# Fewer up products in the last three blocks: 20 matrix products for four column blocks, chained in PSUM banks

## The chip, the cores and the metric

The kernel runs on one core of one Trainium2 chip. The metric is the device time of one execution in microseconds (us). TensorE (PE) multiplies matrices into PSUM, VectorE (DVE) and ScalarE (ACT) read PSUM and work in SBUF, GpSimd (POOL) helps, and SyncE (SP) issues the DMA transfers. PSUM has eight banks of 512 fp32 values per partition.

## The reference

A gated linear attention with a state per head, and behind it a multiplicative feed-forward network on its result:

```
q, k, v, f_logit: (4, 8, 768, 48) float32
f = sigmoid(f_logit)
state = f[t] * state + k[t] (outer) v[t]        # 48 x 48 per head
y[t]  = q[t] @ state
x = y laid out as 3072 tokens x 384
a = x @ w1;  b = x @ w2                         # 384 -> 1024, w1 and w2 float64 in memory
h = (a * b) @ w3                                # 1024 -> 1024
out = h @ w_out                                 # 1024 -> 384
```

The kernel multiplies `w3 @ w_out` once into `wc` (1024 x 384), so that the network is an **up product** of x with w1 and w2, an elementwise product of the two results, and a **down product** with `wc`. All matmuls are fp32.

## The kernel before

The 3072 tokens are six blocks (`NB`, index `n`) of 512 tokens (`TB`). The attention runs in 24 chunks of 128 tokens and delivers each block's x as `xt`: three slices of 128 of the 384 input features (`KM`), by 512 tokens. The up product of a block fills `ab` (the product a * b): eight column blocks of 128 (`KF`) of the 1024 outputs. The down product of a block is two calls of `down(i)`, of 28 matmuls each, in seven runs of four.

**The order of all work is made by a planner.** `Plan.add` takes an engine, a cost, what is waited for and a priority; `Plan.order` goes through the tasks as a list scheduler and puts out one instruction stream per engine. Tasks can take a place from a pool: `f` is a pool of PSUM banks (`NF` = 4), given back when the tasks that end its use are done. The attention holds the other four banks, as two tiles of two banks each, `pa` and `py`. Each engine executes its stream in order.

**How an up product is done.** Block 0 is multiplied plainly (`part`). Blocks 1 to 5 use `seven(jc)`, called four times per block for the column blocks `jc` and `jc + 4`: the tokens are two halves of 256 (`TH`), and a scheme of the Strassen kind takes 11 products of 128x128 by 128x256 in place of 12, in seven groups `m1` to `m7`. Each product is done for w1 and w2 (`both_`, line 901), which land side by side in the two halves of one bank. So a seven has 22 matmuls. `sums` makes four sums of parts of x (VectorE, line 875), and `w12t` holds sums of weights. The results are joined like this (X, Y, Z are banks):

```
m1 -> X;  k1: a = X (ScalarE copy, line 914)
m6 -> Y;  u2 = Y + a (VectorE, line 935);  m2 added to X
k11: ScalarE copies half of X (line 938), e11: VectorE multiplies it by the other half (line 941)
m7 added to Y;  u3 = Y + a (line 935)
m5 -> Z;  c22: u3 += Z (line 953);  e22 (line 956)
m4 added to Y;  c21: a += Y;  e21.   m3 added to Z;  c12: u2 += Z;  e12
```

The `e` steps multiply the w1 half by the w2 half and write `ab`. The down products are lines 805 (matmuls), 1032 (four sums `S0` to `S3`), 1039 to 1083 (copies and adds) and a store of two tiles (line 1088).

**Work that fills ScalarE late.** `ranges` (lines 1309 to 1343) looks at all weights once more after the attention has ended: 34 loads of 512 KB, each followed by two ScalarE passes with a sum (lines 1325 and 1329), at the lowest priority. The verdict on them is awaited by the very last group of matmuls (`m3` of the last `down`).

Of the kernel before, what the change touches and what calls it, by code (L numbers as in the profile page):

```python
# [84 lines left out]
AHEAD = 22.0  # L85
HEAVY = 3
WITH_POOL = 0.6
QLATE = 0.1
FLOOR = 2.0**-60
RANGE = 2.0**-40  # L90

# [139 lines left out]
def ranged(ctx, tc, q, k, f_logit, v, w1, w2, w3, w_out, out, ident, w12, wc, left):  # L231
# [13 lines left out]
    ps = ctx.enter_context(tc.tile_pool(name="ps", bufs=1, space=PSUM))  # L245
    ps_f = ctx.enter_context(tc.tile_pool(name="ps_f", bufs=1, space=PSUM))

    floor = keep.tile([R, NQ], F32, name="floor")
    spare = keep.tile([P, NQ], F32, name="back")
    back = spare[0:R]  # L250
    gate = [keep.tile([R, NQ + 1], F32, name=f"gate{i}") for i in range(2)]
    qs, ks, fs = ([keep.tile([R, NQ], F32, name=f"{nm}{i}") for i in range(n)] for nm, n in (("q", 3), ("k", 2), ("f", 2)))
    both = keep.tile([P, 2 * WIDE], F32, name="A")
    flat = [both[:, i * WIDE : i * WIDE + WIDE] for i in range(2)]
    masked = [t.rearrange("p (r h c) -> p r h c", r=2, h=HP) for t in flat]
# [32 lines left out]
    qs.append(at(12288, NQ)[0:R])  # L288
    dns = {nm: at(12288 + DH * i, DH) for i, nm in enumerate(("m1", "u2", "u3"))}

    plan = Plan()
    plan.pool("f", NF)
    plan.slot("a", 2)
    plan.slot("lane", 8)
    plan.slot("heavy", HEAVY)
    plan.slot("ab", 4)
# [2 lines left out]

    def bank():  # L300

        return ps_f.tile([P, TB], F32, name=f"f{plan.got}")

    def idle(n):

# [80 lines left out]
    def front(u):  # L386

        s, t = st[u], tk[u]
        n0 = need(u)
        ask = n0 - 30 if u in (0, 1) or u > 3 else turn_of(str(u))  # L390
        ask = [ask, ask + 0.5, ask + 1.0, n0 - (28.2, 28.2, 28.2, 28.2, 12)[min(u, 4)] if u in (0, 1) or u > 3 else ask + 1.2]

        def load(dst, src):
            def emit():
                if dst is fs[0] and u == 0:

                    nc.sync.dma_start(dst[0:64], src[u].rearrange("two d n -> (two d) n")[0:64])
                    nc.sync.dma_start(dst[rows(1)], src[u, 1])
                    return
                for par in range(2):  # L400
                    nc.sync.dma_start(dst[rows(par)], src[u, par])  # L401
            return emit

        fu, qu, ku = (x[u if u < 4 else u % n] for x, n in ((fs, 2), (qs, 3), (ks, 2)))

        def free(n, *names):

            if u < 4:
                return []
            return asked[8:9] + [tk[u - n if u - n >= 4 else u % n][nm] for nm in names]  # L410

        since = n0 - AHEAD if 4 < u < 8 else 0.0
        t["lf"] = moves(2, 197, 300, load(fu, f_logit), free(2, "g"), ask[0], since=since)
        t["lk"] = moves(2, 197, 300, load(ku, k), free(2, "k"), ask[1], since=since)
        t["lq"] = moves(2, 197, 300, load(qu, q), free(3, "q"), ask[2], since=since)

        def load_v():
            s["v"] = at(12288 + NQ, DM) if u == 3 else loads.tile([P, DM], F32, name="vt")
            loaded(s["v"], u)

        t["lv"] = moves(
            1, 197, 320, load_v, [] if u == 3 else past(u, 4 if u in (4, 5, 6) else 3, "v", "s"),
            ask[3],
        )

        def gates():
            nc.scalar.activation(gate[u % 2][:, 0:NQ], fu, AF.Sigmoid)  # L427

        t["g"] = plan.add("ACT", 0.65, gates, [t["lf"]] + past(u, 2, "r") + past(u, 3, "G"), n0)
        if u % NCH and "G" in tk[u - 1]:  # L430
            tk[u - 1]["G"]["deps"].append(t["g"])

        def forward():
            s["P"] = one.tile([R, NQ], F32, name="fwd")
            nc.vector.tensor_tensor_scan(s["P"], gate[u % 2][:, 0:NQ], floor, 0.0, ALU.mult, ALU.max)  # L435

        t["p"] = plan.add("DVE", 1.25, forward, [t["g"]] + past(u, 1, "q", "i", "l"), n0)

        def last():
            nc.scalar.copy(lasts[:, u], heads(s["P"])[:, :, C - 1])  # L440

        t["l"] = plan.add("ACT", 0.2, last, [t["p"]], n0)

        def ends():
            nc.vector.reciprocal(heads(back)[:, :, C - 1], heads(s["P"])[:, :, C - 1])

        t["i"] = plan.add("DVE", 0.18, ends, [t["p"]] + past(u, 1, "r"), n0)

        def scale_q():
            s["Q"] = work3.tile([R, NQ], F32, name="Q")  # L450
            nc.vector.tensor_tensor(s["Q"], qu, s["P"], ALU.mult)

        t["q"] = plan.add("DVE", 0.72, scale_q, [t["p"], t["lq"]] + past(u, 3, "v", "a"), n0 + QLATE, shared=True)

        def backward():
            s["R"] = one.tile([R, NQ], F32, name="bwd")
            nc.vector.tensor_tensor_scan(  # L457
                s["R"][:, ::-1], gate[u % 2][:, NQ:0:-1], back[:, ::-1], 0.0, ALU.mult, ALU.max
            )

        t["r"] = plan.add("DVE", 1.25, backward, [t["i"]] + past(u, 1, "k"), n0)

        def scale_k():
            s["K"] = work.tile([R, NQ], F32, name="K")
            nc.vector.tensor_tensor(s["K"], ku, s["R"], ALU.mult)  # L465

        t["k"] = plan.add("DVE", 0.72, scale_k, [t["r"], t["lk"]] + past(u, 2, "a", "t"), n0, shared=True)
        if u in (2, 3):
            t["k"]["frees"].append(coming)
# [207 lines left out]
    def rest(u):  # L677
# [68 lines left out]
                t["b"] = plan.add("ACT", 0.75, blocks, [t["d"]] + past(u, 1, "v"), n0)  # L746

        def outcome():
            s["ys"] = work3.tile([R, HP, C], F32, name="ys")
            py = s["yb"] if u < NPE else s["py"][0:R, :, 0 : 2 * C]  # L750
            ys = s["ys"]
            if u >= NPE:
# [44 lines left out]


    blk = [{} for _ in range(NB)]
    stores, upq, downq = [], [], []  # L800

    def three(out_, lhs, rhs, start=True):

# [6 lines left out]
    def ffn(n):  # L810
# [69 lines left out]
        def seven(jc):  # L880
# [26 lines left out]
                return a_b(jc + half * KH)[:, tok * TH : tok * TH + TH]  # L907

            def m1():
                both_("X", [wt(0, 0)], [quarter(0, 0)], True)  # L910

            def k1():
                q["a"] = firsts[q["no"] % 2]
                nc.scalar.copy(q["a"], q["X"])

            def m6():
                both_("Y", [tw(1)], [xs()[:, 1]], True)

            def m5():
                both_("Z", [tw(0)], [xs()[:, 0]], True)  # L920

            def m2():
                both_("X", [wt(1, 0), wt(2, 0)], [quarter(1, 0), quarter(2, 0)])

            def m7():
                both_("Y", [tw(2), wt(2, 1)], [xs()[:, 2], quarter(2, 1)])
# [4 lines left out]
            def m3():  # L931
                both_("Z", [wt(1, 1), wt(2, 1)], [xs()[:, 3], quarter(2, 0)])

            def u(nm):
                return lambda: nc.vector.tensor_tensor(ups[nm], q["Y"], q["a"], ALU.add)  # L935

            def k11():
                nc.scalar.copy(to(0, 0), q["X"][:, 0:TH])  # L938

            def e11():  # L940
                nc.vector.tensor_tensor(to(0, 0), q["X"][:, TH:TB], to(0, 0), ALU.mult)

            def first():
                return q["a"]

            def second():
                return ups["u2"]

            def third():
                return ups["u3"]  # L950

            def ended(bank_, more):
                return lambda: nc.vector.tensor_tensor(more(), q[bank_], more(), ALU.add)  # L953
# [15 lines left out]

            ready = [tk[n * UB + c]["x"] for c in range(UB)]  # L970
            begin = takes_ab(jc, plan.add("PE", 0.0, lambda: None, ready + [s["S", 3]] + old(1, "m7"), n0))
            pe("m1", one_, m1, [begin], 0, takes=["f"])
            q["k1"] = plan.add("ACT", 0.57, k1, [q["m1"]], -200, takes=["a"])
            pe("m6", one_, m6, [q["m1"]], -1, takes=["f"])
            pe("m5", one_, m5, [q["m6"]], -1, takes=["f"])
            dve("u2", 0.69, u("u2"), [q["k1"], q["m6"]] + old(1, "e12"))
            pe("m2", two_, m2, [q["k1"], q["m6"]], -5)
            q["k11"] = plan.add("ACT", 0.38, k11, [q["m2"]], -200)
            dve("e11", 0.43, e11, [q["m2"], q["k11"]], frees=[q["m1"]])
            pe("m7", two_, m7, [q["u2"], q["m2"]], -5)  # L980
            dve("u3", 0.69, u("u3"), [q["m7"]] + old(1, "e22"))
            dve("c22", 0.69, ended("Z", third), [q["u3"], q["m5"]])
            dve("e22", 0.43, times(1, 1, third), [q["c22"]])
            pe("m4", two_, m4, [q["u3"]], -6)
            dve("c21", 0.69, ended("Y", first), [q["m4"]], frees=[q["m6"]])
            dve("e21", 0.43, times(1, 0, first), [q["c21"]], frees=[q["k1"]])
            pe("m3", two_, m3, [q["c22"], q["m4"]], -6)
            dve("c12", 0.69, ended("Z", second), [q["m3"]], frees=[q["m5"]])
            dve("e12", 0.43, times(0, 1, second), [q["c12"]])
            s["done"][place_of(jc) // KH].extend([q["e11"], q["e22"], q["e21"], q["e12"]])  # L990
            s["up"] += [q[nm] for nm in ("m1", "m2", "m7", "m4", "m3")]

        if n == 0:
            part(0, 2, range(KH))
            part(2, 4, range(KH))
            part(0, 2, range(KH, KF))
# [312 lines left out]
    def ranges():  # L1309
# [19 lines left out]
            return lambda: nc.scalar.activation(a, a, AF.Sign, bias=small, accum_out=counts[:, i : i + 1])  # L1329

        for i in range(n):
            ld = moves(1, LOOK, 400, load(i), last[:1] if i < 2 else last[i - 1 : i], 500 + i, SURE_W)
            a = plan.add("ACT", 0.92, total(i), [ld], 500 + i)
            last.append(plan.add("ACT", 0.95, count(i), [a], 500 + i))

# [40 lines left out]
    for u in range(NU):  # L1376
# [11 lines left out]
        if u == 3:  # L1388
            folding()
        if u == NU - 1:  # L1390
            weighed = [ranges()] if wide else []
            looked = plan.add("DVE", 1.0, judge, [tk[i]["y"] for i in range(NU)] + weighed, -20)
            sent = moves(1, 0.4, 250, told, [looked], 0, 20.0)
# [400 lines left out]
```

## Time and profile before

| what | value |
|---|---|
| median of 3 runs | 474.16 us (473.37 to 476.61) |
| the profiled execution, own time | 473.17 us |
| its span, first to last instruction | 471.4 us |
| mean granted TensorE clock | 0.999 of full |
| TensorE busy | 463.6 us, 98% |
| VectorE busy | 347.0 us, 74% |
| ScalarE busy | 170.2 us, 36% |
| GpSimd busy | 65.5 us, 14% |
| rows of line 901 (sevens' matmuls) | 400 + 240 + 160 + 80 = 880 |
| start of the first look, end of the last (lines 1325, 1329) | about 268 us, 401.6 us |

How to read it: a span is the time from the first to the last instruction. A row of a group names a line of the kernel, the engine, the operation, the output tile and the input tiles, the shapes, how many there were, their busy time and the mean of one in nanoseconds, and then how long the engine had been idle before them and for whom. One fp32 matmul of the program is two MATMUL rows in the trace, and rows of successive matmuls overlap, so that a busy time or a mean is not the rate; the chain of work that ended last gives the rate, as time per row of a stretch without a gap.

The order of the stages by the chain: the attention's start with block 0's up product until 67 us, the fold of w3 and w_out between attention steps until 117 us, the attention with down and up products of blocks 0 and 1 until 264 us, and then only up and down products, block by block.

### The profile page before, as it was taken

What the parts mean: (1) busy time and instruction counts of PE and PEld (TensorE: products, weight loads), DVE (VectorE), ACT (ScalarE), POOL (GpSimd) and SP (SyncE); (2) the same over time, 40 slices, a digit from 0 to 9 for tenths busy, and PEclk for the clock granted to TensorE, in tenths of its full rate; (3) what the DMA queues carried; (4) which work ended last, traced back from release to release, by engine and by line L of the source; (5) the groups of instructions that cost most, each with busy time, mean ns of one, the idle gap of its engine ahead of it and who ended that gap; (6) DMA issues with size and microseconds to landing.
All of it is one profiled execution on the core that took longest, in us unless ns stands there. A gap on an engine that the chain in (4) does not pass through costs nothing.

```text
span 471.4 us, 11711 instructions
## 1 busy us (share of the span) xinstructions
PE 463.6 (98%) x4848; PEld 405.3 (86%) x4848; DVE 347.0 (74%) x615; ACT 170.2 (36%) x398; POOL 65.5 (14%) x90
## 2 busy tenths in 40 slices
PE   8999999999999999999999999999999999999996
PEld 6778885666999888889998889988899888989995
DVE  8998999999898999999986556436672457555541
ACT  4555433432234433233333335454444464200000
POOL 9330000222132332033231000000000000000000
PEclk9999999999999999999999999999999999999999
DMA  6998897643356654164441445554454542000011
GB/s 181 287 293 296 289 346 271 199 117 88 84 150 170 207 140 128 55 186 121 123 116 26 117 137 198 167 171 145 128 194 153 182 136 89 1 0 1 35 66 40
DMA packets 43164, 68.74 MB, mean 146 GB/s; under 512 B 5201, under 2 KB 28242, under 8 KB 42082
## 3 DMA queue, kind: packets, MB, share of 16 engines
q1 hardware_dynamic: 43106, 67.95, 46.3%
q8 instruction: 39, 0.64, 0.6%
q14 instruction: 19, 0.16, 0.1%
HBM read 58.88 MB, written 9.04 MB: 144 GB/s over the span
## 4 chain that ended last, share of the span: by engine, by line
PE 95%; DVE 1%; SPq 1%; DMA 1%; issue 0%; POOL 0%; POOLq 0%; DVEq 0%
PE f L901 41%; PE f L805 32%; PE f L1254 9%; PE py L562 3%; PE pa L488 2%; PE pa L595 2%; PE py L581 2%; PE f L502 2%; PE f L308 1%; SPq L401 1%; DMA ab<-in_k_dram 1%; DVE K L465 0%; PE f L783 0%; DVE bwd L457 0%; DVE fwd L435 0%
## 5 line engine op out<-in xcount | busy, mean ns | idle before, releaser
L901 PE MATMUL f<-xt,w 128*128 128x256 f32 x400 | 103.3, 380 | 0.0
L901 PEld LDWEIGHTS f<-xt,w 128*128 128x128 f32 x400 | 75.4, 190 | 10.0
L901 PE MATMUL f<-place 128*128 128x256 f32 x240 | 63.4, 380 | 0.0
L618 POOL TENSOR_SCALAR_AFFINE_SELECT A<-A 64x512 f32<-64x512 f32 (+1 forms) x46 | 42.5, 924 | 109.2 <-ACT A L612 107.1
L805 PE MATMUL f<-place 128*128 128x192 f32 x288 | 51.2, 328 | 0.0
L901 PEld LDWEIGHTS f<-place 128*128 128x128 f32 x240 | 45.0, 190 | 6.0 <-ACT kt L636 0.2
L805 PEld LDWEIGHTS f<-place 128*128 128x128 f32 x288 | 47.1, 190 | 0.5 <-issue 0.2
L935 DVE TENSOR_TENSOR place<-f,a 128x512 f32<-128x512 f32 x40 | 27.6, 690 | 22.6 <-PE f L901 20.7
L1254 PE MATMUL f<-place 128*128 128x384 f32 x128 | 42.7, 488 | 0.0
L805 PE MATMUL f<-xt,w 128*128 128x256 f32 x192 | 42.1, 380 | 0.0
L805 PEld LDWEIGHTS f<-xt,w 128*128 128x128 f32 x192 | 36.3, 190 | 5.0
L901 PE MATMUL f<-xt,place 128*128 128x256 f32 x160 | 38.1, 381 | 0.0
L1254 PEld LDWEIGHTS f<-place 128*128 128x128 f32 x128 | 23.8, 190 | 15.3
L805 PE MATMUL f<-wc,ab 128*128 128x192 f32 x192 | 35.4, 327 | 0.0
L953 DVE TENSOR_TENSOR place<-f,place 128x512 f32<-128x512 f32 x40 | 27.6, 689 | 9.1 <-PE f L901 8.5
L901 PEld LDWEIGHTS f<-xt,place 128*128 128x128 f32 x160 | 30.0, 190 | 3.9
L805 PEld LDWEIGHTS f<-wc,ab 128*128 128x128 f32 x192 | 31.9, 190 | 0.5
L435 DVE TENSOR_TENSOR_SCAN fwd<-gate,floor 112x512 f32<-112x512 f32 x24 | 31.4, 1307 | 1.3 <-ACT gate L427 0.2
L457 DVE TENSOR_TENSOR_SCAN bwd<-gate,back 112x512 f32<-112x512 f32 x24 | 29.7, 1237 | 0.7
L953 DVE TENSOR_TENSOR a<-f,a 128x512 f32<-128x512 f32 x20 | 13.8, 689 | 21.0 <-PE f L901 21.0
L938 ACT COPY ab<-f 128x256 f32<-128x256 f32 x20 | 7.4, 372 | 58.8 <-PE f L901 58.8
L1329 ACT ACTIVATE A<-A,back 128x512 f32<-128x512 f32 x34 | 26.3, 772 | 1.0
(134 smaller groups left out, 705.8 us busy)
## 6 DMA issues: line engine op xcount, KB each, us to landing
A<-in_w_dram SPq DMA_DIRECT2D x28, 512.0 KB, 4.3
place<-in_w_dram SPq DMA_DIRECT2D x8, 1024.0 KB, 6.4
place<-in_w_dram SPq DMA_DIRECT2D x12, 512.0 KB, 6.7
out_dram<-o SPq DMA_DIRECT2D x24, 192.0 KB, 2.1
q<-in_q_dram SPq DMA_DIRECT2D x46, 96.0 KB, 3.1
vt<-in_v_dram SPq DMA_DIRECT2D x23, 192.0 KB, 3.0
k<-in_k_dram SPq DMA_DIRECT2D x44, 96.0 KB, 2.7
yt<-ys SPq DMA_DIRECT2D x44, 96.0 KB, 2.8
```

Of the source, the lines that this page charges most:

```text
L435: nc.vector.tensor_tensor_scan(s["P"], gate[u % 2][:, 0:NQ], floor, 0.0, ALU.mult, ALU.max)
L457: nc.vector.tensor_tensor_scan(s["R"][:, ::-1], gate[u % 2][:, NQ:0:-1], back[:, ::-1], 0.0, ALU.mult, ALU.max)
L488: nc.tensor.matmul(s["pa"][half * W : half * W + W, par, hp * W : hp * W + W], lhsT=s["K"][rows(par), cols], rhs=s["Q"][rows(par), cols], ...
L502: nc.tensor.transpose(out=s["pk"][:, hp // 2, hp % 2 * R : hp % 2 * R + R], in_=s["K"][:, hp * C : hp * C + C], identity=ident[0:R, 0:R],)
L562: done = nc.tensor.matmul(y_block(u, hp, par, half)[p0 : p0 + w], lhsT=s["v"][half * W : half * W + W, h * D : h * D + w], rhs=s["A"][half ...
L618: nc.gpsimd.affine_select(out=a, in_=a, pattern=pattern, compare_op=ALU.is_ge, fill=0.0, base=0, channel_multiplier=-1,)
L805: nc.tensor.matmul(out_, lhsT=lhs[i], rhs=rhs[i], start=start and i == 0, stop=i == len(lhs) - 1, skip_group_check=True,)
L901: nc.tensor.matmul(q[nm][:, which * TH : which * TH + TH], lhsT=lhs[i](which), rhs=rhs[i], start=start and which == 0 and i == 0, stop=i = ...
L935: return lambda: nc.vector.tensor_tensor(ups[nm], q["Y"], q["a"], ALU.add)
L953: return lambda: nc.vector.tensor_tensor(more(), q[bank_], more(), ALU.add)
L1254: nc.tensor.matmul(w3s["p", jc], lhsT=w3s[jc][:, kc * P : kc * P + P], rhs=wos[:, kc], start=(kc == 0), stop=(kc == KF - 1),)
L1329: return lambda: nc.scalar.activation(a, a, AF.Sign, bias=small, accum_out=counts[:, i : i + 1])
```

## The change

Three things change.

1. **Blocks 3, 4 and 5** (`n >= MANY`, `MANY` = 3) use a new `many(g)` in place of `seven`, called for two groups `g` of four column blocks each. It is a scheme of 20 products for (2 token halves) x (3 feature slices) x (4 column blocks), where a plain product has 24. Each is again done for w1 and w2, so a group has 40 matmuls and a block 80, where four sevens have 88. It needs 12 sums of parts of x per block (`X_SUMS`, VectorE, 128x256), 22 sums of weights once (`W_SUMS`, VectorE, 128x512), 12 sums of products per group (`Y_SUMS`, VectorE, 128x512) and 8 ends per group (`Y_ENDS`). The 20 products stand in six **chains** (`CHAINS`): the products of a chain are added one on the other in one bank, and where a partial sum is needed by itself, ScalarE copies the bank (`keep_`) before the next product of the chain is added; 12 copies per group. One end per group is read from the bank: a half copy by ScalarE and a multiplication by VectorE.
2. **The sevens** of blocks 1 and 2 are chained likewise: `m1` starts bank Y, ScalarE copies it (`k1`), `m6` is added and copied (`u2`), `m7` is added and copied (`u3`), `m4` is added. `m2` starts bank X and `c11` adds the kept m1. So the two additions `u2` and `u3` by VectorE become copies by ScalarE, `m6` waits for `k1`, and the slot `a` has one place.
3. **Space.** The weight sums and kept products live in tiles that the attention has left (`homes`: floor, gates, q, k, f, and the working tiles), which get 128 partitions for it. A task `over` gathers the ends of the attention: the weight sums wait for it. After the attention the banks of `pa` and `py` join the pool `f` (`plan.pools["f"] += [late] * 4`), each bank being a half of one of the two tiles.

`LOOKS`, `W_SINCE` and `W_STEP` are 0 and change nothing by themselves; the planner's costs on TensorE are as before (0.86 for two matmuls). The core of the diff:

```diff
+MANY = 3
+CHAINS = [
+    [(3, 0), (4, 4), (4, 23)],
+    [(0, 13), (1, 6), (1, 26)],
+    [(5, 8), (9, 25), (6, 17), (10, 31)],
+    [(8, 28)],
+    [(11, 14), (12, 22), (3, 19)],
+    [(7, 10), (16, 21), (14, 12), (15, 32), (17, 30), (0, 33)],
+]
...
     def bank():
+        if plan.got >= NF:
+            nm = ("pa", "py")[(plan.got - NF) // 2]
+            if nm not in found:
+                found[nm] = ps.tile([P, 2, NQ], F32, name=nm)
+            return found[nm][:, plan.got % 2]
         return ps_f.tile([P, TB], F32, name=f"f{plan.got}")
...
             def m1():
-                both_("X", [wt(0, 0)], [quarter(0, 0)], True)
-            def k1():
-                q["a"] = firsts[q["no"] % 2]
-                nc.scalar.copy(q["a"], q["X"])
+                both_("Y", [wt(0, 0)], [quarter(0, 0)], True)
+            def m2():
+                both_("X", [wt(1, 0), wt(2, 0)], [quarter(1, 0), quarter(2, 0)], True)
             def m6():
-                both_("Y", [tw(1)], [xs()[:, 1]], True)
+                both_("Y", [tw(1)], [xs()[:, 1]])
-            def u(nm):
-                return lambda: nc.vector.tensor_tensor(ups[nm], q["Y"], q["a"], ALU.add)
+            def kept(to_):
+                return lambda: nc.scalar.copy(to_(), q["Y"])
...
+        def many_sums():
+            for k, (i, o, j, h) in enumerate(W_SUMS if not w_nodes else []):
...
+                w_nodes.append(plan.add("DVE", 0.69, emit, [over] + w_nodes[-1:], 100 * MANY + W_LATE + k, since=W_SINCE + W_STEP * k))
+            for k, (i, o, j, h) in enumerate(X_SUMS):
...
+                s["X", k] = plan.add("DVE", 0.43, emit, before + x_task(i) + x_task(j), 100 * n + 30 + k)
...
+        def many(g):
...
+            def product(t, c, first, a, b):
+                def emit():
+                    if first:
+                        banks[g, c] = bank()
+                    for which in range(2):
+                        lhs = up_weights(w12, which, b // 4, column(b % 4, g)) if b < 4 * KM else w_view(b)[:, which, g]
+                        nc.tensor.matmul(
+                            banks[g, c][:, which * TH : which * TH + TH], lhsT=lhs, rhs=x_node(a),
+                            start=first and which == 0, stop=True, skip_group_check=True,
+                        )
+                return emit
...
+            for c, chain in enumerate(CHAINS):
+                last = None
+                for m, (a, b) in enumerate(chain):
+                    deps = [begin] + x_task(a) + ([w_nodes[b - 4 * KM]] if b >= 4 * KM else []) + ([last] if m else opened[-1:])
+                    task[t] = last = plan.add("PE", 0.86, product(t, c, m == 0, a, b), deps, n0 + 0.1 * c - 0.01 * m, takes=["f"] if m == 0 else [])
...
+                    if t in kept:
+                        def keep_(t=t, c=c):
+                            where_[t] = temporary(plan.got)
+                            nc.scalar.copy(where_[t], banks[g, c])
+                        last = plan.add("ACT", 0.57, keep_, [last], n0 - 200, takes=["t"], frees=[opener] if t in ends_of else [])
...
-        if n == 0:
+        if n >= MANY:
+            for g in range(2):
+                many(g)
+        elif n == 0:
...
         if u == NU - 1:
+            late = plan.add("none", 0.0, lambda: None)
+            plan.pools["f"] += [late] * 4
+            for nm in ("y", "mid", "m", "v"):
+                tk[u][nm]["frees"].append(late)
+            over["deps"] += [tk[u][nm] for nm in ("z", "v", "mid", "k", "q", "y")] + [tk[u - 1]["z"]]
```

## The prediction

> **What bounds the kernel now.** I read the page's busy shares first, then the chain that ended last, then busy time by 12 us stretches, and only then single rows. The page:
>
> ```profile
> PE 463.6 (98%) x4848; PEld 405.3 (86%) x4848; DVE 347.0 (74%) x615; ACT 170.2 (36%) x398; POOL 65.5 (14%) x90
> PE 95%; DVE 1%; SPq 1%; DMA 1%; issue 0%; POOL 0%; POOLq 0%; DVEq 0%
> ```
>
> The second line is the head of the chain: TensorE holds 95% of it. An average can hide a stage with another limit, so here are two stretches of up products in the last three blocks, and the first stretch of all (start:end, length; busy time of each engine, granted clock, DMA):
>
> ```profile
> 0.00:12.00 12.00, 10.10 (x61) 8.18 (x62) 9.63 (x18) 4.99 (x9) 11.01 (x26) 1.00 0.63 181
> ...
> 312.00:324.00 12.00, 12.00 (x57) 10.55 (x57) 6.63 (x12) 5.88 (x15) 0.00 (x0) 1.00 0.40 134
> 324.00:336.00 12.00, 12.00 (x58) 10.55 (x57) 6.42 (x12) 7.70 (x19) 0.00 (x0) 1.00 0.49 174
> ```
>
> In the second and third row TensorE is busy 12.00 of 12.00, VectorE 6.5, ScalarE 6 to 8. From 36 us on every stretch but one reads 12.00 (252 to 264 reads 11.90) until the last products end near 467. So in the last three blocks each TensorE microsecond taken away is one of the kernel, as long as nothing new makes TensorE wait. The chain by time gives the price of a matmul:
>
> ```profile
> 307.88 34.53 PE f L901 x160
> ...
> 364.07 42.30 PE f L901 x196
> ```
>
> 34.53/160 and 42.30/196 are both 0.216 us per row. Each 128x256 fp32 matmul of the program is two rows, so 0.432 us; a product is two of them (w1 and w2 side by side in one bank), 0.863 us. The group's mean of 380 ns is not the price: rows overlap.
>
> **What goes.** Per block, the sevens need 11 products for each of four column pairs, 88 matmuls; the new form 20 for each of two groups, 80. The instruction order shows 24 fewer TensorE instructions in all, all in blocks 3 to 5, and none of another kind added: 24 x 0.432 = **10.36 us**. Before block 1's first seven (149 us) the TensorE order is the same.
>
> **What is added on the other engines.** Rows (out<-in, count, busy, mean ns):
>
> ```profile
> L953 DVE TENSOR_TENSOR place<-f,place 128x512 f32<-128x512 f32 x40 | 27.6, 689 | 9.1 <-PE f L901 8.5
> L956 DVE TENSOR_TENSOR ab<-place 128x256 f32<-128x256 f32 x40 | 17.0, 425 | 1.3
> L914 ACT COPY a<-f 128x512 f32<-128x512 f32 x20 | 11.7, 586 | 31.5 <-PE f L901 31.5
> L1325 ACT ACTIVATE A<-A 128x512 f32<-128x512 f32 x34 | 23.1, 678 | 7.0 <-DMA A<-in_w_dram 5.9 <-DMA A<-in_w_out_dram 1.0
> ```
>
> VectorE, per block: before, 4 x (5 x 0.69 + 4 x 0.425) + 4 x 0.42 = 22.2 us; after, 24 sums of products (0.69), 16 ends (0.425), 12 sums of x (0.42) = 28.4. Over three blocks +18.6, and once 22 weight sums, 15.2. The chained sevens of blocks 1 and 2 give back 2 x 0.69 each, 11.0. Net +22.8 us on an engine with 5 us free in 12 there: no bound on average.
>
> ScalarE, per block: before 4 x (0.586 + 0.372) = 3.8; after 24 x 0.586 + 2 x 0.372 = 14.8, so +33. Each chained seven adds 1.17, +9.4. ScalarE also does the 34 looks at the weights in this time (lines 1325 and 1329 with their accumulator reads: 0.678 + 0.189 + 0.773 + 0.187 = 1.83 each).
>
> All of this is off the chain unless TensorE waits for it, so the waits have to be priced.
>
> **The chain step.** A product that adds to a bank whose partial sum is kept may start only when ScalarE's copy is done. No row shows that very wait under pressure; the nearest is the first copy of a seven:
>
> ```profile
> 307.72 1.03 PE L901 MATMUL f<-xt,w 128*128 128x256 f32 x4
> ...
> 308.78 0.58 ACT L914 COPY a<-f 128x512 f32<-128x512 f32 x1 [2.73 <-PE f L901]
> ```
>
> The four rows are one product. It stops issuing at 307.72 + 0.863 = 308.58, and the copy starts 0.20 us later. 0.20 + 0.586, plus 0.04 to wake TensorE and a weight load of 0.19 that is then uncovered, is a loop of **1.02 us**. I set it against the TensorE work that stands between a product and its successor in the built order:
>
> - 59 of 89 such steps have two products between, 1.73 us: 0.71 us to spare. Those with more are safe, and so are five with 1.26 to 1.30.
> - Short ones: one in block 1 has 0.86. In the last blocks two more have 0.86, one has 0.00. These come from the banks: the four late ones are halves of two tiles, `pa` and `py`, and the built waits take such a tile as one. In block 5 the copy of `py`'s second half waits for a matmul into its first half, and the next matmul into the first half waits for that copy. Cost 1.02 + 3 x 0.16 = **1.5 us**.
> - 26 of the 1.73 us steps have a look directly ahead of their copy in ScalarE's queue. A look's half takes up to 0.96; it hurts only by what exceeds 0.71. Were every one caught at its very start, 26 x 0.25 = 6.5 us; were none, 0. With the rest of the look spread evenly over 0 to 0.96, 26% are caught for 0.125 on average: **0.9 us**, taken.
>
> Behind a waiting matmul stands all of TensorE's queue; behind a late copy stand the next copies and down's copies on ScalarE.
>
> **VectorE's latest stretch.** Weight sums may start only when the attention has ended. The weight sum for `bwd` is the 20th: 35.0 us of VectorE work in its order stand from the first weight sum to it, and 41.9 us of TensorE work from the place where the first is reached to the product that reads `bwd`. Almost 7 us to spare, with VectorE some 84% busy. Other waits, such as opening a bank that a VectorE sum has still to read: between 0 and 3 us, **0.6** taken, nearer zero because the order puts block 2's down products (1.30 us each four matmuls) into this stretch.
>
> **End of the kernel.** After the last up product eight runs of block 4's down products (10.4 us) stand before the first that reads block 5's result, and only one 0.43 us VectorE end is left over. No new tail. The last look stands 58 us ahead of the end by TensorE work (the trace has 401.6 of 471.4, 70 us, before): the verdict is not late. DMA queues carry the same transfers; the work of POOL and of the attention is the same.
>
> **A rule against the change.** The Trainium skill, "TensorE: Matmul & The Clock Gate", section "A second HAM failure mode: psum-queue depth-cycling": micro-idles between matmul groups as PSUM banks are cycled can make the clock fall back to half. Chaining adds just such micro-idles. By the rule, a fall for one window of about 3.4 us costs 1.7 us, so four short steps would make some 7 us (an estimate from that page). The row that bears on it is 0:12 above: TensorE idle for 1.9 of 12 us and clock 1.00, as in all stretches. By the row, 0, which I take; 7 us stays as an end of the range.
>
> **Sum** against the profiled execution, 473.17 us (span 471.4): 473.17 - 10.36 + 1.5 + 0.9 + 0.6 = **465.8 us**. The median of three runs is 474.16, one of them 476.61; I make no correction for that and predict 465.8. About 1%, 4.7 us, is what a measurement of this kernel tells from no change.
>
> **Rivals.**
> - *All waits hidden*: 473.17 - 10.36 = 462.8. For it: today chain steps at 1.73 us, and one at 1.30, with a 0.69 us VectorE add inside, stall nowhere. Against: the 0.00 step cannot be hidden. Chance 0.17.
> - *Halves of one tile*: 33 matmuls into `pa` or `py` wait for ScalarE in the new products. If holding each other up costs each 0.2 us, that is 6.6 us: 469.4 and hardly a change. Against: most of these waits still have 1.73 us. Or VectorE starts its weight sums 14 us later than I place them, 7 more than it can spare: 469.8. Together 0.16.
> - *Slower: looks in ScalarE's queue*. ScalarE executes in order, and a look whose 512 KB transfer is late holds back the copies behind it; in the row of line 1325 looks waited 6.9 us for DMAs, harmlessly because one copy per seven stood behind. Now three in five products wait for a copy. 29 look pairs stand between the first and last such copy; at 10.36/29 = 0.36 us each the gain is gone, at 0.6 each the time is 480.2. Against: only 6 of 34 pairs waited at all, and a ScalarE slowed by copies asks for its loads later. Chance 0.05.
> - *The clock falls*: 465.8 + 7 = 472.8, no change. Chance 0.02.
> - The likeliest, some 1.5 to 6 us of new stalls, 464.3 to 468.8: 0.60.
>
> That the change might not do what it says is excluded by the order: 80 matmuls per block.
>
> The range, 462.5 to 471.0, holds the likeliest case, the hidden one and the nearer half of the second. Faster by over 1% (below 469.4): the likeliest, the hidden one and half of the second rival, 0.85. Within 1%: 0.10. Slower: 0.05.
>
> **What would show it.** Right: matmul rows fall by 48, chain rows of the new products keep 0.216 us each, TensorE idle in the last 200 us between 1.5 and 6 us and pinned on ScalarE's copies, VectorE near 10 of 12 us after the attention, clock 1.00, the last stretch as dense as now. Wrong: windows with TensorE below 11 of 12 us, long waits for looks' DMAs on ScalarE with TensorE idle, or a clock below 1.00.

## The result, and the profile after

| | before | after |
|---|---|---|
| median, us | 473.93 (473.37 to 476.61, 4 runs) | 466.71 (465.51 to 467.52, 4 runs) |
| profiled execution, us | 473.17 (span 471.4) | 466.62 (span 464.9) |
| end of the last matmul | 466.96 | 459.92 |
| start of the first seven's matmul | 149.9 | 150.7 |

The ratio is 0.9838 (95% interval 0.98 to 0.9875). The predicted 465.8 lies 0.8 us below the profiled execution. The busy line of the page after, and the head of its chain:

```profile
PE 454.4 (98%) x4800; PEld 396.0 (85%) x4800; DVE 364.9 (78%) x657; ACT 206.8 (44%) x468; POOL 64.6 (14%) x90
PE 94%; POOL 2%; DVE 1%; issue 1%; ACT 0%; POOLq 0%; DVEq 0%
```

48 rows fewer on TensorE, 42 instructions more on VectorE, 70 more on ScalarE: the amounts that the order gave. The 12 us stretches (start:end, length; busy time of PE, PEld, DVE, ACT, POOL; granted clock, DMA share, GB/s):

```profile
0.00:12.00 12.00, 10.26 (x60) 8.47 (x61) 9.65 (x18) 5.21 (x9) 11.01 (x26) 1.00 0.66 183
...
264.00:276.00 12.00, 12.00 (x57) 10.56 (x56) 11.38 (x20) 7.35 (x19) 0.00 (x0) 1.00 0.49 165
...
312.00:324.00 12.00, 12.00 (x61) 10.84 (x60) 6.05 (x14) 6.55 (x16) 0.00 (x0) 1.00 0.49 164
324.00:336.00 12.00, 12.00 (x57) 10.32 (x56) 7.64 (x15) 8.08 (x19) 0.00 (x0) 1.00 0.40 132
...
372.00:384.00 12.00, 11.07 (x52) 9.31 (x50) 7.87 (x14) 7.73 (x18) 0.00 (x0) 1.00 0.38 118
384.00:396.00 12.00, 11.32 (x53) 9.61 (x52) 7.40 (x15) 8.86 (x21) 0.00 (x0) 1.00 0.31 93
```

In the two stretches that the prediction showed, 312 to 336, TensorE is as full as before, with VectorE and ScalarE near their old levels. Before them stand the weight sums (line 1075, 261.6 to 298.4 us): VectorE is busy 11.38 of 12 there, and TensorE still 12.00. Two stretches, 372 to 396, have holes of 0.93 and 0.68 us. The waits of TensorE from 140 us on name them (engine, tile, line; waited for; us in all, times, longest):

```profile
PE pa L1114 <- ACT ys L1135: 0.9, 1, 0.9
PE py L1114 <- ACT Q L1135: 0.7, 1, 0.7
```

Line 1114 is the new products, line 1135 ScalarE's copies of kept partial sums. The chain in order of time shows how each came about (start, us, what):

```profile
370.97 1.74 PE pa L1114 x8
...
372.74 0.03 ACT Q L1135
...
373.22 0.75 ACT A L1517 x2
373.97 0.48 ACT ys L1135
...
374.50 1.99 PE pa L1114 x8
...
383.40 0.88 PE py L1114 x4
384.27 0.02 issue
384.30 0.59 ACT Q L1135
...
384.94 1.99 PE py L1114 x8
386.93 0.86 PE f L1114 x4
```

The second hole is the one step of 0.00 us that the prediction found: the product ends at 384.27, its copy takes 0.59, and TensorE starts again at 384.94. In the first, two products into `pa` (x8 is two products) are both waited for by copies; between the copies stands a look (line 1517), and the next product into `pa` comes only after the second copy. TensorE has one product into `f` to do meanwhile, so by the prediction's own measure this is a step of 0.86. Even the first copy is late: ScalarE stands idle until both products have ended, where in e1_halves (below), with each bank a tile of its own, the same copy starts behind the first:

```profile
372.74 0.58 ACT L1135 COPY Q<-pa 128x512 f32<-128x512 f32 x1 [1.14 <-PE pa L1114]
```

```profile
371.06 0.59 ACT L1139 COPY Q<-l 128x512 f32<-128x512 f32 x1 [0.28 <-PE l L1118]
```

The first line is the changed kernel's, the second that of e1_halves; in brackets stands the idle time before. Outside the holes the price is the old one: the x4 and x8 rows of this chain have 0.86 and 1.73, 0.216 us per row.

From the first seven to the end of the last matmul, 317.1 us became 309.2: 7.84 less (from unrounded starts), where the matmuls alone should give 10.36. So 2.5 us of new stalls: 1.6 in the two waits, 0.5 in the uncovered starts behind them (1.99 in place of 1.73, twice), and some 0.4 left, of which the trace names only late weight loads of 0.4 us and less. In this execution the first seven started 0.8 later, though TensorE's order before it is the same, and the tail behind the last matmul is 4.98 us in place of 4.44. Together -10.36 + 2.5 + 0.8 + 0.54 = -6.5, which is the difference of the spans.

### The profile page after: what moved, and what is told of

The parts are those of the page before. It is cut to its first block, busy times and chain, and to the rows that moved or that the text cites. A ratio compares the mean times of both kernels' runs of the same rounds, so it can differ in the third digit from the quotient of the medians.

```text
span 464.9 us, 11763 instructions
## 1 busy us (share of the span) xinstructions
PE 454.4 (98%) x4800; PEld 396.0 (85%) x4800; DVE 364.9 (78%) x657; ACT 206.8 (44%) x468; POOL 64.6 (14%) x90
## 4 chain that ended last, share of the span: by engine, by line
PE 94%; POOL 2%; DVE 1%; issue 1%; ACT 0%; POOLq 0%; DVEq 0%
PE f L863 25%; PE f L959 14%; PE f L1114 12%; PE f L1446 9%; PE pa L1114 5%; PE py L1114 5%; PE py L863 5%; PE pa L863 3%; PE py L619 3%; PE pa L545 2%; PE pa L652 2%; PE f L559 2%; PE py L638 2%; PE pa L959 1%; POOL ab L403 1%; PE f L365 1%
## 5 line engine op out<-in xcount | busy, mean ns | idle before, releaser
L863 PE MATMUL f<-xt,w 128*128 128x256 f32 x192 | 42.1, 380 | 0.0
L863 PEld LDWEIGHTS f<-xt,w 128*128 128x128 f32 x192 | 36.3, 190 | 5.0
L1446 PEld LDWEIGHTS f<-place 128*128 128x128 f32 x128 | 23.8, 190 | 15.3
L959 PE MATMUL f<-xt,w 128*128 128x256 f32 x132 | 34.2, 379 | 0.0
L863 PE MATMUL f<-place 128*128 128x192 f32 x184 | 33.9, 329 | 0.0
L863 PEld LDWEIGHTS f<-place 128*128 128x128 f32 x184 | 30.1, 190 | 0.8 <-DVE place L1237 0.3
L959 PEld LDWEIGHTS f<-xt,w 128*128 128x128 f32 x132 | 24.8, 190 | 3.1
L1384 ACT ACTIVATE place<-place 128x512 f32<-128x512 uint32 (+2 forms) x24 | 21.1, 890 | 9.9 <-DMA place<-in_w_dram 7.6
L1517 ACT ACTIVATE A<-A 128x512 f32<-128x512 f32 x34 | 23.3, 685 | 4.0 <-DMA A<-in_w_dram 4.0
L959 PE MATMUL f<-place 128*128 128x256 f32 x84 | 22.4, 385 | 0.0
L484 ACT ACTIVATE gate<-f 112x512 f32<-112x512 f32 x22 | 13.9, 632 | 15.8 <-DMA f<-in_f_logit_dram 5.6
L619 PEld LDWEIGHTS py<-A,vt 64*64 64x64 f32 (+1 forms) x672 | 13.3, 127 | 7.3 <-issue 5.7
L619 PE MATMUL py<-A,vt 64*64 64x64 f32 (+1 forms) x672 | 18.1, 223 | 0.2
```

The source lines that it names most:

```text
L619: done = nc.tensor.matmul(y_block(u, hp, par, half)[p0 : p0 + w], lhsT=s["v"][half * W : half * W + W, h * D : h * D + w], rhs=s["A"][half ...
L863: nc.tensor.matmul(out_, lhsT=lhs[i], rhs=rhs[i], start=start and i == 0, stop=i == len(lhs) - 1, skip_group_check=True,)
L959: nc.tensor.matmul(q[nm][:, which * TH : which * TH + TH], lhsT=lhs[i](which), rhs=rhs[i], start=start and which == 0 and i == 0, stop=i = ...
L1384: nc.scalar.activation(lo.bitcast(F32), lo, AF.Copy, bias=2.0, scale=2.0**-51)
L1446: nc.tensor.matmul(w3s["p", jc], lhsT=w3s[jc][:, kc * P : kc * P + P], rhs=wos[:, kc], start=(kc == 0), stop=(kc == KF - 1),)
L1517: return lambda: nc.scalar.activation(a, a, AF.Abs, accum_out=sums_[:, i : i + 1])
```

## The experiments

Two theories of the 2.5 us stood against each other. **A:** the late banks are halves of two tiles, `pa` and `py`, and are waited for as one tile, so a product in one half waits for a copy of the other half. **B:** ScalarE is held up by its looks at the weights, and its copies come late. A third question was whether VectorE had the spare time that the prediction claimed.

### e1_halves: four late banks as tiles of their own

```diff
-    ps = ctx.enter_context(tc.tile_pool(name="ps", bufs=1, space=PSUM))
+    ps_stack = ctx.enter_context(ExitStack())
+    ps = ps_stack.enter_context(tc.tile_pool(name="ps", bufs=1, space=PSUM))
...
-            nm = ("pa", "py")[(plan.got - NF) // 2]
+            if "late" not in found:
+                ps_stack.close()
+                found["late"] = ctx.enter_context(tc.tile_pool(name="ps_late", bufs=1, space=PSUM))
+            nm = f"l{plan.got}"
             if nm not in found:
-                found[nm] = ps.tile([P, 2, NQ], F32, name=nm)
-            return found[nm][:, plan.got % 2]
+                found[nm] = found["late"].tile([P, TB], F32, name=nm)
+            return found[nm]
```

> The changed kernel with one edit: after the attention the four late banks are four tiles of one bank each, in place of the halves of pa and py; every engine keeps its order. The built waits then have no chain step with less than 0.86 us of TensorE work between in the last three blocks. Theory A (a two-bank tile is waited for as one, and that makes the stalls of 0.9 us before a pa product near 374.5 and of 0.7 us before a py product near 384.9): the py stall goes entirely, 0.95 us with its uncovered weight load; the pa stall, which also has a look between the two copies, shrinks by about half, 0.5 us. 466.7 - 1.5 = 465.2 us, and the stretch from the first seven to the last down product 307.6 in place of 309.07. Rival B (the looks in ScalarE's queue make both stalls): no change, 466.5 to 466.9, stretch 309.0.

Measured: 463.19 us (462.61 to 463.64), ratio to before 0.9773 (0.976 to 0.9787). TensorE's order is that of the changed kernel; only the waits differ. From 140 us on no wait of TensorE for a copy is left, and the stretches that had holes are full:

```profile
372.00:384.00 12.00, 12.00 (x57) 10.58 (x56) 9.07 (x18) 9.71 (x23) 0.00 (x0) 1.00 0.36 97
384.00:396.00 12.00, 12.00 (x57) 10.56 (x56) 7.88 (x15) 8.94 (x21) 0.00 (x0) 1.00 0.41 128
```

First seven to end of the last matmul: 306.4 us, 10.6 less than before, against 10.36 from the matmuls. So all that the change lost in this stretch, it lost to the tiles: the loss of 2.5 us is gone, where theory A had expected 1.5 of it to go. This version beats both kernels, by 3.5 us against the medians of the changed one.

### e2_no_looks and e3_halves_no_looks: without ScalarE's looks

```diff
-            weighed = [ranges()] if wide else []
+            weighed = []
...
-        if wide:
-            nc.vector.tensor_tensor(good, good, where["weights"], ALU.mult)
```

Both leave out the 34 loads, their ScalarE passes and the verdict on the weights; the second has the tiles of e1_halves too.

> The changed kernel without the 34 looks at the weights after the attention (this part of the check on the inputs is left out); the planner then orders the last blocks anew. Theory A: the pa stall loses its look, the py one stays where such a step is still in the order; 0.5 to 1.0 us less, 465.7 to 466.2. Rival B: all stalls of the last 200 us go, 2.5 us, 464.2. A third case, that ScalarE was no cause at all: 466.7.

> Both edits together (the looks left out, four late tiles). Theory A and B agree: no short step and no look is left, so the stretch from the first seven to the last down product should be 316.91 - 10.36 = 306.55 us plus at most 0.5 of other waits, and the time 466.7 - 2.0 to 2.5 = 464.2 to 464.7 us. If it stays above 465.5, part of the missing gain has another cause (VectorE, or the sevens).

Measured: 464.65 (464.36 to 465.2), ratio 0.9809 (0.9795 to 0.9822), and 463.14 (462.76 to 464.55), ratio 0.978 (0.9763 to 0.9797). With two-bank tiles and no looks neither of the two waits shows; another one does, at 338 us (first line below). Near 372 us, where the changed kernel had products in `pa`, the chain now has nine products in a row in `f` (second line):

```profile
PE pa L1114 <- ACT ys L1135: 0.3, 1, 0.3
```

```profile
370.32 7.77 PE f L1114 x36
```

The stall falls from 2.5 to some 1.1 us, and the time lies nearer to rival B's 464.2 than to A's 465.7 to 466.2. But the planner made another order here, with other banks, so this run can't tell the looks' part from the order's; looks taken out with the order kept were not run. With tiles of their own, taking the looks away gains 0.05 us: nothing (both times are below the 464.2 to 464.7 that was expected of this kernel). So the looks alone cost nothing in these three blocks. That they lengthen a wait that exists only because two banks are one tile is read from the chain above, where 0.75 us of a look stands between the two copies. A is the cause, shown by e1_halves with the order kept; B is at most an amplifier here.

### e4_weight_sums_twice: what VectorE had to spare

```diff
-                    nc.vector.tensor_tensor(w_view(4 * KM + k), w_view(i), w_view(j), op(o))
+                    homes_in = [W_SUMS[x - 4 * KM][3] for x in (i, j) if x >= 4 * KM]
+                    twice = k < 22 and W_SUMS[k][3] not in homes_in
+                    for _ in range(1 + twice):
+                        nc.vector.tensor_tensor(w_view(4 * KM + k), w_view(i), w_view(j), op(o))
```

A sum that overwrites one of its operands can't be repeated: 15 of the 22 are, 15 x 0.69 = 10.4 us more on VectorE, with the order of all engines kept.

> The changed kernel with 15 of the 22 weight sums done twice in place (the result of a sum is written again), same order on every engine: 10.4 us more on VectorE, 6.9 of them ahead of the sum for bwd. If VectorE had almost 7 us to spare there, as the prediction had it, the time rises by 0 to 4 us: 6.9 is just covered, the whole 10.4 is 3.5 over it; 466.7 to 470.5. If its sums are already what the products wait for, all of it appears: 477.

Measured: 474.22 (473.41 to 474.5), ratio 1.0006 (0.9997 to 1.0014). First seven to last matmul grew by 8.2 us against the changed kernel. So some 2.2 us were free, not almost 7. TensorE's waits tell for whom it came late:

```profile
PE py L959 <- DVE place L1009: 3.4, 1, 3.4
PE pa L959 <- DVE a L1009: 1.7, 1, 1.7
PE pa L863 <- DVE ab L1006: 1.2, 1, 1.2
```

None of these is a product that reads a weight sum (line 1117 here). Line 959 is block 2's sevens, line 863 down products: they wait for VectorE instructions that stand behind weight sums in its order. All three go to halves of `pa` or `py`, and this was not run with tiles of their own, so how much of the 8.2 us the shared tiles add is open.

### e10_weight_sums_twice_planned: the same work, known to the planner

```diff
-                w_nodes.append(plan.add("DVE", 0.69, emit, [over] + w_nodes[-1:], ...
+                w_nodes.append(plan.add("DVE", 1.38, emit, [over] + w_nodes[-1:], ...
```

> As e4_weight_sums_twice (weight sums done twice but for one of them, 474.22), and the planner is told: their cost in the list scheduler is 1.38 us instead of 0.69, so the order of all engines is made with the doubled work in it. If VectorE has no room for 10.4 us more, the time stays near 474. If only the order had no room, and other products can be put ahead of those that wait: within 3 us of the changed kernel, 466.7 to 469.5.

(15 sums are repeated here too, not all but one.) Measured: 469.5 us (468.78 to 469.71), ratio 0.9904 (0.9882 to 0.9926). The same 10.4 us now cost 2.8 against the changed kernel's median. First seven to last matmul is 3.3 us longer than in the changed kernel. The waits for VectorE are now 1.2 us at most (lines 1227 and 1240 are sums and adds of the down products):

```profile
PE f L863 <- DVE place L1227: 1.2, 1, 1.2
PE py L863 <- DVE place L1240: 1.1, 2, 0.6
```

The spare time of an order is not that of the work: with the cost in the plan, VectorE does adds of block 2's sevens ahead of weight sums that stood before them (the last sums start after 296 us; in e4_weight_sums_twice they had ended at 291.3), TensorE's order is another from about 283 us on, and the waits of 3.4 and 1.7 us are gone.

### e5_chained_sevens_only and e9_halves_sevens_only: chaining alone

```diff
-MANY = 3
+MANY = 6
```

No block takes the new products; all twenty sevens are chained and, once the attention has ended, use the late banks, as do down products. The second has the tiles of e1_halves besides.

> Only the sevens of blocks 1 and 2 (and, as no block takes the new products, of 3 to 5 too) are chained; the 20-product scheme and its weight sums are not done. Each seven keeps its 22 matmuls and loses two VectorE adds (1.38 us) for two ScalarE copies. Theory of the prediction (TensorE alone bounds the blocks after 36 us, so work taken from VectorE is worth nothing): 473.5 us, ratio 1.00 within 0.3%. Rival 1, the step from m1 through the copy k1 to m6 costs TensorE: with two products (m2, 1.73 us) between them it should not, but at 0.2 us for each of 20 sevens it would be 477.5. Rival 2, VectorE's relief is itself a gain: 471 or less.

> As e5_chained_sevens_only (477.58: chained sevens in blocks 1 to 5, no product less, sevens and down products using the four late banks), but the late banks are four tiles of one bank each. If the 3.7 us that e5_chained_sevens_only loses come from the two-bank tiles, they go, and with as many matmuls as before: 473.5 to 474. If they come from the chaining (m6 waiting for k1, the copies on ScalarE): 477 still. Below 472 if chained sevens with more banks gain by themselves.

Measured: 477.58 (477.13 to 477.69), ratio 1.0071 (1.0052 to 1.0089), and 474.34 (473.11 to 477.5), ratio 1.0012 (0.9998 to 1.0027). The first hits the number of "the wait for k1 costs 0.2 us a seven" and is still no evidence for it. The chain shows one of the places where that kernel loses time:

```profile
360.48 2.61 PE pa L863 x16
...
363.12 0.37 DVE place L1250
...
363.53 1.58 PE pa L863 x8
...
365.14 0.37 DVE o L1261
...
365.55 1.57 PE pa L863 x8
```

Down products in a row into the halves of `pa`: two runs, then VectorE's add of one half, then one run, then the next add. What should overlap goes in turn. With four separate tiles and the same chaining, 3.2 us of the 3.7 are gone and the rest is within what can't be told from no change. No cost of the chaining can be told from nothing, and relief for VectorE, whose busy time fell from 347.0 to 321.7 us, buys nothing.

### e6_halves_many_only: the new products without chained sevens

```diff
-    plan.slot("a", 1)
+    plan.slot("a", 2)
...
-                both_("Y", [wt(0, 0)], [quarter(0, 0)], True)
+                both_("X", [wt(0, 0)], [quarter(0, 0)], True)
...
-            act("u2", 0.57, kept(second), [q["m6"]] + old(2, "e12"))
+            dve("u2", 0.69, u("u2"), [q["k1"], q["m6"]] + old(1, "e12"))
...
-            act("u3", 0.57, kept(third), [q["m7"]] + old(1, "e22"))
+            dve("u3", 0.69, u("u3"), [q["m7"]] + old(1, "e22"))
```

> The four late banks are tiles of their own, as in e1_halves (463.19), and the sevens of blocks 1 and 2 are as in the kernel before (their two VectorE adds kept, slot a with two places). The number of matmuls is the same as in e1_halves. VectorE gets 1.38 us per seven back, some 4 of the sevens standing in the stretch in which the 22 weight sums are done. If the weight sums have little to spare there, as e4_weight_sums_twice showed (10.4 us more cost 8.2, so some 2 us were free), 4 x 1.38 = 5.5 us use that up and cost 3.4: 466.6. If the chaining of the sevens carries nothing: 463.2. Below 463 if the wait for k1 was a cost.

Measured: 463.85 (463.54 to 464.27), ratio 0.9779 (0.9744 to 0.9814). The 3.4 us that I expected from the small spare of e4_weight_sums_twice did not come; no wait of TensorE shows from 130 us on. The order was made anew with the adds in it, as in e10_weight_sums_twice_planned, and the banks are tiles of their own; which of the two hid the adds is open. The 0.66 us over e1_halves hardly stand clear of the spread: the two ranges overlap. In the profiled executions (spans 462.5 and 461.9) the first seven starts 0.1 later, the stretch to the last matmul is 306.6 in place of 306.4, and the rest is the tail, where the chain goes through the verdict:

```profile
456.23 0.15 DVE left L1568
...
457.25 0.36 DVE o L1278
```

The last matmul ends at 456.92, and this last add starts 0.33 us later; in e1_halves it starts 0.04 later.

### e7_halves_one_block and e8_halves_four_blocks: how many blocks

```diff
-MANY = 3
+MANY = 5      # e7; 2 in e8
```

Both have the tiles of e1_halves. With the border between the forms moved, by the built order, in each of them one seven's sum reads a tile that a kept product of the new form has already overwritten, so these two do not compute the reference's values. The instructions are those described, but a wait that would keep the two apart is missing.

> As e1_halves, but only block 5 takes the new products (MANY = 5), blocks 3 and 4 use chained sevens: 8 matmuls fewer instead of 24. If each matmul that goes is worth 0.432 us and nothing else counts: 473.5 - 3.45 = 470.1. If a part of the gain of e1_halves came from elsewhere (the chained sevens, the banks that are freed), it is below 469.5; if the 22 weight sums, which are done for one block alone here, cost more than nothing, above 470.5.

> As e1_halves, but block 2 takes the new products too (MANY = 2): 32 matmuls fewer instead of 24. If the slope holds: 463.2 - 3.45 = 459.7. Against it: the weight sums can start only when the attention has ended, and block 2's products that read them come soon after; e4_weight_sums_twice showed only some 2 us to spare for the adds queued behind them. If TensorE has to wait there for the sums, 15.2 us of VectorE work come ahead of the first blocks' products: anything from 461 to 470.

Measured for one block: 470.47 (470.14 to 470.81), ratio 0.9918 (0.9891 to 0.9945), that is 3.4 us below before's 473.88, against 8 x 0.432 = 3.45. By the interval it could be 2.6 to 5.2, so the price of a matmul holds as far as this run can tell.

For four blocks: 484.36 (482.15 to 486.51), ratio 1.0199 (1.0139 to 1.0258), slower than before and far over my 461 to 470. The stretch of the attention's end, in steps of 4 us:

```profile
212.00:216.00 4.00, 3.33 (x63) 2.41 (x66) 3.72 (x8) 1.49 (x3) 1.22 (x3) 1.00 0.39 107
216.00:220.00 4.00, 3.10 (x87) 2.54 (x77) 2.69 (x4) 2.32 (x6) 1.96 (x2) 1.00 0.57 161
220.00:224.00 4.00, 2.64 (x16) 2.32 (x15) 3.36 (x7) 0.32 (x1) 0.00 (x0) 1.00 0.68 186
...
244.00:248.00 4.00, 3.13 (x106) 2.70 (x110) 3.76 (x8) 0.89 (x4) 1.71 (x2) 1.00 0.54 154
248.00:252.00 4.00, 1.94 (x65) 1.47 (x55) 3.93 (x8) 1.70 (x4) 2.02 (x2) 0.97 0.25 53
252.00:256.00 4.00, 3.44 (x106) 3.13 (x99) 1.49 (x5) 0.72 (x3) 0.00 (x0) 0.50 0.00 0
256.00:260.00 4.00, 2.00 (x48) 1.63 (x52) 3.38 (x6) 0.55 (x1) 1.64 (x2) 0.50 0.65 171
...
264.00:268.00 4.00, 0.13 (x1) 0.00 (x0) 0.60 (x1) 2.53 (x6) 0.00 (x0) 1.00 0.64 197
268.00:272.00 4.00, 0.86 (x2) 0.78 (x3) 3.90 (x8) 2.51 (x7) 0.00 (x0) 0.60 0.61 183
272.00:276.00 4.00, 4.00 (x11) 3.17 (x11) 3.90 (x7) 1.30 (x3) 0.00 (x0) 0.55 0.55 183
```

and TensorE's waits from 200 to 300 us:

```profile
PE f L1118 <- DVE fwd L1079: 7.0, 1, 7.0
PE py L623 <- POOL A L679: 4.6, 6, 1.5
```

Here the 7.0 us wait is for a weight sum (line 1079): block 2's new products come straight after the attention. But the sums are late for a reason of their own. The chain leads back to a look (lines 1521 and 1525):

```profile
260.82 3.90 DMA A<-in_w_dram
...
264.80 0.75 ACT A L1521 x2
...
266.88 0.50 ACT place L1139
...
267.40 0.70 DVE place L1162
...
271.14 6.78 PE f L1118 x20
```

The look waits for its transfer, two copies wait behind the look, VectorE's add (line 1162) waits for the copies, idle for 4.6 us, and four weight sums stand behind the add in VectorE's order. The products that the copies read have ended by 264.1, so without this look I estimate the sums some 2.5 us earlier. That is the mechanism of the prediction's rival "looks in ScalarE's queue", in a kernel whose banks are tiles of their own: the looks cost nothing with three blocks, but they delay TensorE here.

The rest I had not seen: sevens of block 2 were work that filled TensorE around the attention's last small steps (in e1_halves 18 of their rows run between 240 and 252 us, and 50 between 252 and 264; here there are none), and products that need weight sums can't fill there, as the sums wait for the attention's end. TensorE then waits for POOL's masks (line 679), and the granted clock falls to 0.50. The waits shown are 11.6 of the 24.6 us that are lost (21.2 against e1_halves, and the 3.45 of the matmuls that went); the remainder was not taken apart. Four blocks would need another order or another place for the looks.

## Why the prediction was right, point by point

- **What goes.** Confirmed: 48 rows, 0.216 us each in the new products too; 10.6 us in e1_halves, where no wait of TensorE is left, and 3.4 for a third of it in e7_halves_one_block.
- **What is added.** The counts were right. The page's busy time grew less than the sums of means: 17.9 us on VectorE where 22.8 was forecast, 36.6 on ScalarE where 42 was. Instructions back to back overlap by some 0.1 us in the trace, and busy time counts that once.
- **The chain step.** The step of 0.00 was priced at 1.02 us. Its gap is 384.94 - 384.27 = 0.67, and the two products behind it take 1.99 in place of 1.73: 0.93. Its cause, two halves waited for as one tile, was right. The hole at 372 us is a step of 0.86, for which the prediction's price without a look was 0.16: it cost a gap of 0.93 and 0.26 behind it, 1.2 us.
- **Looks ahead of copies.** Priced at 0.9 us as a term of its own, over 26 steps. No such step shows a wait, and e3_halves_no_looks shows that without the shared tiles the looks cost 0. The look that did hurt stood at a short step, the one at 372 us: the first copy of `pa` waits for both halves, and the look comes between it and the second. So the two terms were one, and that their sum, 2.4 us, met 2.5 is in part luck. The whole sum is near in the same way: the 0.6 us of other waits did not come, and 1.3 us of later start and longer tail were in no term.
- **VectorE.** The 0.6 us of other waits did not come: no wait of TensorE itself for VectorE is named from 140 us on, only weight loads 0.4 us and less. The "almost 7 us to spare" failed as a step. It was measured to the product that reads `bwd`; the work that comes late first is block 2's sevens behind the same queue, with some 2.2 us free by e4_weight_sums_twice. That is the spare time of this order with two-bank tiles. It cost nothing because the change itself needed none of it, though VectorE was busy 10.5 to 11.4 of 12 us from 264 to 312, more than the 84% assumed.
- **The end.** No new wait, as said; the 0.54 us of longer tail and 0.8 us of later start were in no term. In e1_halves the first seven starts at 150.2, only 0.3 later than before, so I take most of the 0.8 for run to run.
- **The rule against it.** The Trainium skill, "TensorE: Matmul & The Clock Gate", section "A second HAM failure mode: psum-queue depth-cycling", is about micro-idles such as the chains make, seen there in a bf16 kernel; the prediction's estimate from that page was some 7 us. With holes of 0.93 and 0.68 us in the stretches 372 to 396 the clock stayed at 1.00; 0 was right. e8_halves_four_blocks shows the clock falling to 0.50, but only after 8 us in which TensorE was busy for 5.07.
- **The rivals.** "All waits hidden" (462.8) is what the change would have been with separate tiles: 463.19. "Halves of one tile" had the right mechanism, but its 33 waits at 0.2 us were far too many: two waits made most of the 2.5 us. Looks' DMAs made ScalarE wait 4.0 us in all, less than before, and none of TensorE's two waits leads back to one; in e8_halves_four_blocks one does.

## What to carry to other kernels

When banks are lent out one by one, give each a tile of its own: with two banks in one tile, the built program lets a write to one wait for a read of the other, which cost 2.8 us here (stretch of the traces) with one form of products and 3.2 (medians) with another. Slack on a queue is to be measured to the nearest consumer of anything that stands behind the new work, and it is the slack of that order only; telling the planner the cost won back most of it. Before work is moved out of a stage, ask what idle time it was filling: the fourth block saved 3.45 us of matmuls and cost 21 us against e1_halves.

## What the runs showed of the hardware

The granted clock stays at 1.00 with TensorE busy 10.26 of the first 12 us, in the changed kernel's holes of 0.93 and 0.68 us, and in e8_halves_four_blocks with 9.07 busy of the 12 us from 212 on. In that run it reads 0.50 from 252 to 260 us, after 3.13 and 1.94 busy of 4 us each, and 0.60 and 0.55 in the two stretches that follow one with 0.13 busy of 4. From 276 us on it is at 1.00 again.
